# Forming the low halves of the first four units with TensorE and ScalarE, loading early on one queue, and ordering the first ten units anew

## The chip, the core and the metric

The kernel runs on one core of a Trainium2 chip. The metric is device time in microseconds (us), from three timed runs of the kernel before; beside it stands one profiled execution, whose rows are read below. TensorE multiplies matrices into PSUM, VectorE (DVE in the rows) and ScalarE (ACT) work element by element and can read PSUM, GpSimd (POOL) works on SBUF only, SyncE (SP) issues transfers.

## What is computed

A recurrent attention over 768 steps feeds two dense blocks in a row. All matrix products are asked for in float32 quality.

```python
for t in range(S):                       # B 4, H 8, S 768, D 48
    cur = einsum('bhd,bhe->bhde', u * k[t], v[t])
    y[t] = einsum('bhd,bhde->bhe', r[t], state + cur)
    state = w[t][..., None] * state + einsum('bhd,bhe->bhde', k[t], v[t])
x = y as (B*S = 3072 tokens, 384)
h = x @ w_in                             # 384 x 1024
solu = h * softmax(h)
ln = (solu - mean) / sqrt(var + 1e-6) * g_ln
x2 = ln @ w_out                          # 1024 x 384
out = leaky_relu(x2 @ w_in2, 0.01) @ w_out2   # 384 x 2048, 2048 x 384
```

## The kernel before

The 3072 tokens are 24 units of 128 tokens; unit i is the batch row i % 4 in the chunk i // 4 of the sequence. Each unit passes through three stages. The attention: `prep1` to `prep4`, `prep_k`, `prep_diag` on VectorE make decayed keys and queries, `prep_bonus`, `prep_vd`, `prep_state` on GpSimd the rest, `att_kt`, `att_scores`, `att_u`, `att_y` are small matmuls, and `att_x` (L624, L625) adds up the unit's activations x. The first dense layer: x is turned by TensorE (`x_t`, L630), then split into a high half (`x_hi`, L635, a ScalarE copy of PSUM to float32r) and a low half (`x_lo`, L639, VectorE: PSUM minus the high half), and multiplied in three passes per slice, high by high, high by low, low by high (`mm1`, L647, 9 matmuls of 512 columns for each half of the 1024 columns, into the one PSUM tile PH). The activation: `soft_max` (L652), `soft_e` (L655), `soft_z` (L659), which is the last reader of PH, `soft_nm` (L663, GpSimd), `soft_c` (L667), `soft_q` (L670); z is turned (`z_t`, L677, into PZ) and split in two halves (`z_hi`, L686, ScalarE; `z_lo`, L690, VectorE, 512 columns each). Groups of three units go through the second layer (`mm2a`, `mm2b`, L700; `mm2_out`, L705). From unit 4 on each unit carries one such product of an earlier group, so units 0 to 3 have less TensorE work than the rest.

The weights arrive as 64-bit floats and are decoded to float32 on the chip: for each of 14 slices of the first block, `w1_a` (L195 on VectorE, L197 on ScalarE), `w1_e` (L201), `w1_f` (L206), `w1_h` (L212), `w1_b` (L217), all VectorE. `w1_c` copies the high half (L783) and forms the difference in PSUM by an identity matmul (L785) and a matmul with minus the identity (L786); `w1_d` (L792) copies it out. This decoding runs between the first six units; the second block's weights follow later.

Nothing orders the work but the text: `FIRST` (units 0 to 9 and the weights), `LOOP` (units 10 to 13) and `LAST` are lists of step names, run in that order, and each engine executes its own instructions in the order in which they were issued. SyncE issues the loads of keys, queries and decays (`load_tr`, L460, two buffers), of values (`load_nat`, L466 and L467), of the second weight (`load_o`, L725) and of u and g. ScalarE issues the three loads of the first weight (`load_w1`, L715) at the start. `minus` is minus the identity, `ident` the identity. After the last unit the second block runs over 512-token groups (`mm3`, L895; `mm4`, L924).

Of the kernel before, what the change touches and what calls it, by code (L numbers as in the profile page):

```python
# [50 lines left out]
att_scores 3; x_hi 2; w1_a; w1_d; w1_f; w1_a; x_lo 2; soft_c 1; w1_e; soft_q 1; w1_h; prep_k 4; w1_b; prep3 4; mm1 2
0; w1_e; mm1 2 1; w1_c; w1_h; w1_f; w1_b; w1_h; z_t 1; att_kt 4; w1_d; w1_f; w1_b; z_hi 1 0; att_evac_s 3; load_nat
5; prep_check 4; w1_a; z_lo 1 0; att_evac_k 4; prep4 4; prep1 5; w1_c; prep_state 5; z_hi 1 1; prep_vd 3; att_u 4;
prep_k 5; w1_h; att_scores 4; z_lo 1 1; w1_d; soft_max 2; att_y 3; w1_c; soft_e 2; att_kt 5; w1_d; att_mid 4; att_x
3; x_t 3; att_mul_next 4; w1_b; prep_bonus 4; x_hi 3; soft_z 2; x_lo 3; prep2 5; w1_c; mm1 3 0; att_evac_s 4;
soft_nm 2; w1_e; att_state 4; w1_f; soft_c 2; w1_h; z_t 2; prep_diag 4; soft_q 2; z_hi 2 0; mm1 3 1; w1_b; z_hi 2 1;
att_evac_k 5; prep_vd 4; w1_d; load_tr 6; z_lo 2 0; w1_c; load_nat 6; att_u 5; prep_check 5; z_lo 2 1; att_y 4;
w1_d; prep3 5; prep4 5; att_scores 5; prep1 6; att_mid 5; mm2a 4; att_x 4; soft_max 3; prep_k 6; prep2 6; x_t 4;
load_tr 7; prep_bonus 5; soft_e 3; soft_z 3; x_hi 4; x_lo 4; mm2b 4; att_mul_next 5; prep_diag 5; soft_nm 3; mm1 4
0; mm2_out 4; soft_c 3; z_t 3; att_state 5; prep3 6; att_kt 6; prep_vd 5; att_evac_k 6; load_nat 7; prep1 7; prep_k  # L60
7; z_hi 3 0; att_evac_s 5; z_hi 3 1; prep_check 6; prep2 7; z_lo 3 0; z_lo 3 1; prep4 6; prep_state 6; mm2a 5; mm1 4
1; soft_max 4; prep_bonus 6; soft_q 3; prep_bonus 7; soft_e 4; load_tr 8; att_y 5; att_u 6; prep_check 7; att_x 5;
att_mid 6; att_scores 6; att_evac_s 6; att_kt 7; x_t 5; att_evac_k 7; mm2b 5; x_hi 5; soft_z 4; x_lo 5; soft_nm 4;
soft_c 4; prep3 7; att_mul_next 6; mm1 5 0; z_t 4; prep1 8; prep_diag 6; z_hi 4 0; z_lo 4 0; z_hi 4 1; prep_state 7;
att_state 6; prep4 7; prep_check 8; load_nat 8; prep_vd 6; mm1 5 1; mm2_out 5; z_lo 4 1; att_scores 7; att_u 7;
soft_max 5; att_y 6; prep2 8; prep_diag 7; att_x 6; att_evac_s 7; mm2a 6; soft_q 4; soft_e 5; x_t 6; prep_k 8;
att_mid 7; load_tr 9; soft_z 5; prep_bonus 8; x_hi 6; soft_nm 5; load_nat 9; soft_c 5; x_lo 6; prep3 8; mm2b 6;
prep4 8; mm2_out 6; att_mul_next 7; prep1 9; prep_vd 7; mm1 6 0; z_t 5; mm1 6 1; prep2 9; att_state 7; z_hi 5 0;
att_kt 8; z_lo 5 0; z_hi 5 1; mm2a 7; load_tr 10; z_lo 5 1; prep_diag 8; prep_k 9; att_evac_k 8; soft_max 6; att_y
7; att_u 8; load_nat 10; soft_q 5; prep_state 8; prep3 9; att_scores 8; att_kt 9; att_x 7; soft_e 6; x_t 7; att_mid  # L70
8; prep_bonus 9; x_hi 7; prep4 9; soft_z 6; prep_state 9; x_lo 7; mm2b 7; att_evac_k 9; mm1 7 0; att_mul_next 8;
att_evac_s 8; soft_nm 6; soft_c 6; z_t 6; soft_q 6; prep_vd 8; prep1 10; prep_diag 9; z_hi 6 0; mm1 7 1; z_lo 6 0;
prep_k 10; z_hi 6 1; att_state 8; mm2_out 7; att_u 9; prep_check 9; z_lo 6 1; att_scores 9; att_y 8; mm2a 8; att_mid
9; soft_max 7; soft_e 7; load_nat 11; att_x 8; x_t 8; x_hi 8; prep_check 10; prep_bonus 10; mm2b 8; soft_z 7; x_lo
8; mm1 8 0; prep2 10; prep_vd 9; soft_nm 7; prep3 10; att_mul_next 9; att_evac_s 9; prep_diag 10; load_tr 11; soft_c
7; prep1 11; z_t 7; prep4 10; att_kt 10; z_hi 7 0; att_evac_k 10; prep_k 11; z_hi 7 1; prep_bonus 11; z_lo 7 0; z_lo
7 1; mm1 8 1; att_state 9; soft_max 8; mm2_out 8; prep_state 10; load_tr 12; soft_q 7; soft_e 8; att_scores 10;
att_y 9; att_x 9; soft_z 8; prep2 11; att_u 10; att_evac_s 10; prep3 11; prep_vd 10; soft_nm 8; mm2a 9; soft_c 8;
att_mid 10; x_t 9; x_hi 9; load_nat 12; x_lo 9; prep_diag 11; mm2b 9; prep_check 11; att_mul_next 10; z_t 8; mm1 9
0; z_hi 8 0; z_lo 8 0; prep1 12; prep4 11; z_hi 8 1; prep_k 12; att_kt 11; mm2_out 9; att_evac_k 11; z_lo 8 1;  # L80
# [1011 lines left out]
```

## Time and profile before

| | us |
|---|---|
| median of three timed runs | 766.18 |
| lowest, highest | 765.87, 768.52 |
| the profiled execution, its own time | 766.61 |
| its span, first to last instruction | 764.9 |
| TensorE busy in the span | 722.2 (94%) |
| VectorE busy | 513.3 (67%) |
| ScalarE busy | 354.0 (46%) |
| GpSimd busy | 155.1 (20%) |

Busy time is an average over stages that differ: the first 100 us and the last 360 us have different limits. So the rows below are cut by stretch. A row of a timeline gives start, duration, engine, line and operation; on VectorE the next row usually starts 0.08 us before the end of the one before, so a step costs its duration less 0.08.

### The profile page before, as it was taken

The page shows a single profiled execution, that of the slowest core. Times are in us where ns is not written, and L with a number is a line of the kernel's source. Part 1 is how long each engine was busy: PE and PEld are TensorE (multiplying, and loading weights), DVE is VectorE, ACT ScalarE, POOL GpSimd, SP SyncE. Part 2 cuts the span into 40 slices and gives each one's busy share as a digit, 9 for nine tenths or more (in the row PEclk, how much of TensorE's full clock was granted, in tenths as well). Part 3 has the DMA queues.
Part 4 walks back from the last instruction along what each step waited for, and adds up shares of the span by engine and source line. Part 5 has one row for each costly group of instructions (what it writes and reads, how often), then busy time and mean ns, then how long its engine had stood idle before and what let it go on. Part 6 is the DMA issues. An engine that isn't in the chain of part 4 may idle for free.

```text
span 764.9 us, 14969 instructions
## 1 busy us (share of the span) xinstructions
PE 722.2 (94%) x6197; PEld 610.7 (80%) x6197; DVE 513.3 (67%) x866; ACT 354.0 (46%) x648; POOL 155.1 (20%) x181
## 2 busy tenths in 40 slices
PE   2588999999999999998999999999999999999996
PEld 1355878989998989887888888888888888888885
DVE  6999889778888888877989976353343334334332
ACT  3567565566565655566555544323322332332231
POOL 2331544355553444312000100001000100100000
PEclk9999999999999999999999999999999999999998
DMA  9652325353444443223363220040020001001001
GB/s 298 214 166 68 105 80 177 91 151 105 137 135 131 131 147 110 65 84 114 114 227 104 73 72 1 1 165 1 1 81 2 1 0 43 0 1 42 0 1 44
DMA packets 30189, 66.60 MB, mean 87 GB/s; under 512 B 3228, under 2 KB 15668, under 8 KB 29988
## 3 DMA queue, kind: packets, MB, share of 16 engines
q1 hardware_dynamic: 29300, 62.45, 25.9%
q10 hardware_dynamic: 816, 3.15, 1.2%
q8 instruction: 50, 0.82, 0.5%
q14 instruction: 23, 0.19, 0.1%
HBM read 56.13 MB, written 9.45 MB: 86 GB/s over the span
## 4 chain that ended last, share of the span: by engine, by line
PE 88%; DVE 7%; DMA 2%; issue 1%; ACT 1%; POOL 0%; ACTq 0%; DVEq 0%; POOLq 0%
PE PK L895 13%; PE PZ L895 13%; PE PH L647 12%; PE PO L700 11%; PE PA L924 9%; PE PH L924 9%; PE PO L924 4%; PE PZ L924 4%; PE PZ L677 2%; PE PZ L609 2%; PE PA L700 2%; DMA zh<-in_w1p_dram 2%; PE PA L546 2%; PE PZ L618 1%; PE PA L566 1%
## 5 line engine op out<-in xcount | busy, mean ns | idle before, releaser
L915 DVE TENSOR_TENSOR gw<-t,gh 128x512 fp32r<-128x512 f32 x96 | 68.4, 713 | 52.6 <-ACT gh L911 52.4
L911 ACT CAST gh<-t 128x512 fp32r<-128x512 f32 x96 | 59.6, 621 | 67.3 <-DVE t L907 51.5
L907 DVE TENSOR_TENSOR t<-t,PZ 128x512 f32<-128x512 f32 x48 | 32.9, 686 | 68.8 <-ACT t L903 68.6
L907 DVE TENSOR_TENSOR t<-t,PK 128x512 f32<-128x512 f32 x48 | 33.0, 687 | 60.0 <-ACT t L903 59.8
L881 POOL TENSOR_TENSOR x2l<-x2l,x2h 128x1536 fp32r<-128x1536 f32 x4 | 14.1, 3532 | 287.4 <-ACT x2h L877 287.4
L903 ACT ACTIVATE t<-PZ 128x512 f32<-128x512 f32 x48 | 28.7, 598 | 83.6 <-PE PZ L895 78.7
L903 ACT ACTIVATE t<-PK 128x512 f32<-128x512 f32 x48 | 28.7, 598 | 80.7 <-PE PK L895 76.4
L647 PE MATMUL PH<-w1ih,xh 128*128 128x512 f32 x144 | 58.7, 407 | 4.0 <-DVE zbuf L659 3.4
L700 PE MATMUL PO<-zh,w1oh 128*128 128x384 f32 x168 | 60.0, 357 | 0.0
L647 PE MATMUL PH<-w1ih,xl 128*128 128x512 f32 x144 | 57.3, 398 | 0.8 <-DVE xl L639 0.8
L647 PE MATMUL PH<-w1il,xh 128*128 128x512 f32 x144 | 56.8, 394 | 0.0
L700 PE MATMUL PO<-zh,w1ol 128*128 128x384 f32 x168 | 56.3, 335 | 0.0
L700 PE MATMUL PO<-zl,w1oh 128*128 128x384 f32 x168 | 56.3, 335 | 0.0
L895 PE MATMUL PK<-x2h,w2ih 128*128 128x512 f32 x144 | 56.2, 390 | 0.0
L895 PE MATMUL PZ<-x2h,w2il 128*128 128x512 f32 x144 | 56.1, 389 | 0.0
L895 PE MATMUL PZ<-x2l,w2ih 128*128 128x512 f32 x144 | 56.1, 389 | 0.0
L895 PE MATMUL PK<-x2h,w2il 128*128 128x512 f32 x144 | 56.0, 389 | 0.0
L895 PE MATMUL PK<-x2l,w2ih 128*128 128x512 f32 x144 | 56.0, 389 | 0.0
L895 PE MATMUL PZ<-x2h,w2ih 128*128 128x512 f32 x144 | 56.0, 389 | 0.0
L655 ACT ACTIVATE ebuf<-PH,nmax 128x1024 f32<-128x1024 f32 x24 | 26.8, 1117 | 38.9 <-DVE nmax L652 38.6
L652 DVE TENSOR_REDUCE nmax<-PH 128x1 f32<-128x1024 f32 x24 | 29.3, 1219 | 13.7 <-PE PH L647 13.6
L690 DVE TENSOR_TENSOR zl<-PZ,zh 128x512 fp32r<-128x512 f32 x48 | 31.8, 682 | 8.5 <-ACT zh L686 8.4
(183 smaller groups left out, 1943.2 us busy)
## 6 DMA issues: line engine op xcount, KB each, us to landing
tr<-in_trw_dram SPq DMA_DIRECT2D x23, 675.9 KB, 5.4
natq<-in_nat_q_dram SPq DMA_DIRECT2D x24, 384.0 KB, 5.3
w2s<-in_moe_w_in_dram SPq DMA_DIRECT2D x48, 128.0 KB, 2.2
w2s<-in_moe_w_out_dram SPq DMA_DIRECT2D x16, 384.0 KB, 3.1
...
```

What stands on the lines that cost most here:

```text
L546: pe.matmul(out=PA[64 * c:64 * c + 64, x, 64 * a:64 * a + 64], lhsT=kt[p:q, 2 * a + c], rhs=lt[p:q, 2 * a + c], start=True, stop=True)
L647: pe.matmul(out=PH[:, half], lhsT=a[:, kc], rhs=c[:, kc, 512 * half:512 * half + 512], start=(n == 0), stop=(n == 8))
L652: dve.tensor_reduce(out=nmax[:, i:i + 1], in_=flat(PH), axis=AX.X, op=ALU.max, negate=True)
L655: act.activation(out=ebuf, in_=flat(PH), func=AF.Exp, bias=nmax[:, i:i + 1], accum_out=s_all[:, i:i + 1])
L690: dve.tensor_tensor(out=zl, in0=p, in1=f(zh), op=ALU.subtract)
L700: pe.matmul(out=o2[m], lhsT=a[:, c, 128 * m:128 * m + 128], rhs=d[:, c], start=(c == 0 and q == 0), stop=(c == K1 - 1 and q == 2))
L895: pe.matmul(out=h_at[n % 2], lhsT=a[:, kc, 128 * o:128 * o + 128], rhs=d[:, kc], start=(q == 0), stop=(q == 8))
L903: act.activation(out=gs[n][0], in_=h_at[n % 2], func=AF.Copy, scale=0.01)
L907: dve.tensor_tensor(out=t, in0=t, in1=h_at[n % 2], op=ALU.max)
L911: act.copy(out=gh, in_=t)
L915: dve.tensor_tensor(out=gw, in0=t, in1=f(gh), op=ALU.subtract)
L924: pe.matmul(out=at, lhsT=a[:, c % 4, 128 * o:128 * o + 128], rhs=d, start=(c == 0 and q == 0), stop=(c == K2 - 1 and q == 2))
```

## The change

For units 0 to 3 (`N_PE` = 4) the low halves of x and z are no longer made by VectorE. After the high half is copied out, TensorE adds minus that half onto the turned values in PSUM (`x_lm`, one matmul of 384 columns; `z_lm`, one of 512 for each half), and ScalarE copies what is left to the low half. The turning matmuls get explicit start and stop flags so that their PSUM group can be added to. `prep_k` goes to GpSimd from unit 2 on instead of from unit 5 on. The loads of the first weight move from ScalarE's queue to SyncE's (`load_w`), the first of them ahead of unit 0's `load_tr`, and the `FIRST` order places all early loads. `load_tr` takes 1552 columns instead of 1545, cut at 528 instead of 521 for unit 0. `FIRST` has the same steps otherwise, in a new order.

```diff
+TRL = 1552
+N_PE = 4
 FIRST = """
-load_tr 1; prep1 0; prep2 0; w1_a; load_nat 0; prep3 0; prep_k 0; w1_e; load_u; w1_f; prep4 0; att_scores 0; w1_a;
-w1_a; w1_h; w1_e; prep_state 0; w1_e; w1_b; w1_f; w1_f; att_kt 0; w1_h; w1_c; prep1 1; w1_h; w1_b; prep_check 0;
-prep2 1; w1_b; prep3 1; w1_a; w1_a; w1_a; prep_k 1; w1_e; w1_e; att_evac_k 0; w1_d; prep_bonus 0; w1_f; att_u 0;
...
-prep_check 2; prep2 3; att_x 1; att_state 2; prep_bonus 2; w1_h; x_t 1; soft_max 0; x_hi 1; prep_diag 2; load_tr 4;
-soft_e 0; prep_vd 2; prep3 3; att_kt 3; prep_state 2; w1_g; soft_z 0; w1_f; load_nat 3; soft_nm 0; soft_c 0; x_lo 1;
...
+w1_a; prep1 0; load_w 1; prep_state 0; w1_e; prep2 0; load_w 2; load_tr 1; w1_f; prep_check 0; prep3 0; prep_k 0;
+w1_h; att_kt 0; prep4 0; w1_a; w1_a; w1_b; w1_e; w1_e; w1_f; w1_c; w1_d; att_evac_k 0; load_o 0; w1_f; w1_h; w1_h;
+w1_a; w1_a; w1_b; w1_e; w1_c; w1_b; w1_e; load_g; load_nat 0; load_u; att_u 0; w1_a; prep1 1; w1_f; load_nat 1;
...
+prep_vd 1; att_kt 2; load_nat 2; w1_d; prep_state 2; w1_a; mm1 0 1; att_evac_k 2; prep1 3; prep_check 3; att_y 1;
+att_u 2; prep4 2; soft_max 0; att_x 1; w1_e; load_tr 4; prep_k 3; soft_e 0; x_t 1; att_mid 2; att_scores 2; soft_z
+0; w1_f; att_evac_s 2; w1_g; w1_h; prep_bonus 2; x_hi 1; x_lm 1; x_lo 1; mm1 1 0; prep_check 4; w1_h; soft_nm 0; mm1
...
 """
-        def load_tr(i, eng, cuts=(0, TRW)):
-            t = ap2.tile([128, TRW], F32, name="tr", bufs=2)
+        def load_tr(i, eng, cuts=(0, TRL)):
+            t = ap2.tile([128, TRL], F32, name="tr", bufs=2)
...
-            (dve if i < 5 else pool).tensor_tensor(
+            (dve if i < 2 else pool).tensor_tensor(
...
+        def turn(out, x, n, of):
+            pe.matmul(out=out, lhsT=x, rhs=ident, is_transpose=True, start=(n == 0), stop=(n == of - 1),
+                      skip_group_check=True)
+
+        def x_lm(i):
+            pe.matmul(out=PZ[0][:, 0:384], lhsT=minus, rhs=flat(xhl[i][0]), start=False, stop=True,
+                      skip_group_check=True)
+
+        def z_lm(i, hb):
+            pe.matmul(out=PZ[hb], lhsT=minus, rhs=z_views(i, hb)[0], start=False, stop=True, skip_group_check=True)
...
-            dve.tensor_tensor(out=xl, in0=PZ[0][:, 0:384].rearrange("p (k t) -> p k t", k=KC), in1=f(xh),
-                              op=ALU.subtract)
+            p = PZ[0][:, 0:384].rearrange("p (k t) -> p k t", k=KC)
+            if i < N_PE:
+                act.copy(out=xl, in_=p)
+            else:
+                dve.tensor_tensor(out=xl, in0=p, in1=f(xh), op=ALU.subtract)
...
-            dve.tensor_tensor(out=zl, in0=p, in1=f(zh), op=ALU.subtract)
+            if i < N_PE:
+                act.copy(out=zl, in_=p)
+            else:
+                dve.tensor_tensor(out=zl, in0=p, in1=f(zh), op=ALU.subtract)
...
-        def load_w1():
-            for hf in range(2):
-                t = ma.tile([128, K1 * 384], I32, name="zl" if hf else "zh")
-                for a, n in ((0, 1), (1, 2)) if hf == 0 else ((0, 3),):
-                    act.dma_start(
...
+        def load_w(n):
+            hf, a, k = ((0, 0, 1), (0, 1, 2), (1, 0, 3))[n]
+            t = w1_at[hf] = w1_at.get(hf) or ma.tile([128, K1 * 384], I32, name="zl" if hf else "zh")
+            sp.dma_start(
...
-            load_tr(0, sp, (0, 521, TRW))
-            load_w1()
+            load_w(0)
+            load_tr(0, sp, (0, 528, TRL))
```

Two facts of the new order are used below, both read off the two lists. Up to and with `soft_z 3`, VectorE has 13 instructions fewer and none more: `x_lo` of units 0 to 3, `z_lo` of units 0 to 2 (two each) and `prep_k` of units 2 to 4. Up to and with `mm1 4 0`, TensorE has the same steps and ten more: `x_lm` of units 0 to 3 and `z_lm` of units 0 to 2 (two each).

## Rows read from the trace of the kernel before

**Rows 1.** Busy us by stretch: PE, PEld, DVE, ACT, POOL; granted clock, DMA share, GB/s.

```profile
13.10:51.90 38.80, 23.96 (x291) 15.22 (x287) 38.19 (x66) 20.94 (x43) 12.83 (x13) 1.00 0.63 217
51.90:98.00 46.10, 41.87 (x533) 32.82 (x533) 41.32 (x78) 30.36 (x61) 13.77 (x19) 0.93 0.32 98
98.00:168.60 70.60, 69.06 (x969) 61.49 (x969) 59.67 (x91) 42.25 (x83) 32.96 (x42) 1.00 0.39 121
168.60:400.00 231.40, 228.46 (x2805) 204.27 (x2805) 195.43 (x339) 133.79 (x253) 78.53 (x89) 1.00 0.41 127
400.00:764.90 364.90, 357.80 (x1579) 295.94 (x1577) 172.28 (x283) 124.27 (x207) 14.13 (x4) 0.99 0.10 34
```

**Rows 2.** The chain that ended last, 50 to 101 us: start, us, what.

```profile
50.62 1.21 DVE zbuf L659 x2
51.87 0.73 PE PH L647 x2
...
58.66 2.09 PE PH L647 x9
...
98.06 2.33 PE PH L647 x9
```

**Rows 3.** Timeline of VectorE, 6 to 14 us, the rows that waited for transfers.

```profile
6.00 1.24 DVE L478 TENSOR_TENSOR_SCAN suf<-tr,sel 112x520 f32<-112x520 f32 x1 [3.81 <-DMA tr<-in_trw_dram]
...
9.60 0.69 DVE L489 TENSOR_TENSOR kt<-tr,suf 112x512 f32<-112x512 f32 x1 [0.68 <-DMA tr<-in_trw_dram]
...
13.02 0.43 DVE L195 TENSOR_SCALAR ebuf<-zh 128x512 int32<-128x512 int32 x1 [1.06 <-DMA zh<-in_w1p_dram]
```

**Rows 4.** Timeline of VectorE, 38 to 69 us: `x_lo`, `z_lo`, `prep_k`, their successors.

```profile
38.03 0.55 DVE L639 TENSOR_TENSOR xl<-PZ,xh 128x384 fp32r<-128x384 f32 x1
38.50 0.20 DVE L484 RECIPROCAL e<-suf 112x8 f32<-112x8 f32 x1
...
59.70 1.29 DVE L690 TENSOR_TENSOR zl<-PZ,zh 128x512 fp32r<-128x512 f32 x2 [0.72 <-ACT zh L686]
60.90 1.22 DVE L652 TENSOR_REDUCE nmax<-PH 128x1 f32<-128x1024 f32 x1
...
68.72 0.69 DVE L489 TENSOR_TENSOR kt<-tr,suf 112x512 f32<-112x512 f32 x1
```

**Rows 5.** Groups by line and form, 0 to 98 us: busy us, mean ns | idle before.

```profile
L667 ACT ACTIVATE zbuf<-zbuf,nm_all 128x1024 f32<-128x1024 f32 x3 | 3.4, 1149 | 2.4 <-POOL nm_all L663 2.4
L686 ACT CAST zh<-PZ 128x512 fp32r<-128x512 f32 x6 | 3.3, 592 | 0.2 <-PE PZ L677 0.2
L635 ACT CAST xh<-PZ 128x384 fp32r<-128x384 f32 x5 | 2.4, 474 | 1.2 <-PE PZ L630 1.2
L489 POOL TENSOR_TENSOR kt<-tr,suf 112x512 f32<-112x512 f32 x2 | 2.4, 1184 | 3.7 <-PE PZ L609 3.7
```

**Rows 6.** Stretches of the start, columns as in rows 1; GB/s is last.

```profile
0.00:2.50 2.50, 0.00 (x0) 0.00 (x0) 1.11 (x4) 0.26 (x1) 1.64 (x10) 1.00 0.17 25
2.50:5.00 2.50, 0.00 (x0) 0.00 (x0) 0.00 (x0) 1.42 (x3) 1.20 (x7) 1.00 0.92 287
5.00:7.50 2.50, 0.00 (x0) 0.00 (x0) 1.47 (x3) 0.00 (x0) 0.00 (x0) 1.00 1.04 349
7.50:10.00 2.50, 0.00 (x0) 0.00 (x0) 1.82 (x3) 0.72 (x1) 0.00 (x0) 1.00 1.04 305
...
10.00:20.00 10.00, 4.57 (x39) 2.43 (x39) 8.90 (x16) 3.53 (x7) 1.68 (x2) 1.00 1.02 364
...
37.50:40.00 2.50, 2.11 (x13) 1.45 (x9) 2.50 (x6) 1.36 (x3) 0.52 (x1) 1.00 1.02 394
```

**Rows 7.** Timeline of VectorE and GpSimd, 25 to 30 us: one step with and without GpSimd.

```profile
25.88 0.42 DVE L206 TENSOR_SCALAR zl<-zl 128x512 int32<-128x512 int32 x1
...
29.08 1.00 POOL L521 TENSOR_TENSOR natq<-natq 128x384 f32<-128x384 f32 x1
29.25 1.11 DVE L206 TENSOR_SCALAR zl<-zl 128x512 int32<-128x512 int32 x1
```

More of the change, by code (lines that the diff above doesn't have):

```diff
@@ L51 @@
[L51 to L80, printed above, removed]
@@ new lines @@
+prep_k 4; att_x 2; att_state 2; att_evac_k 3; w1_c; x_t 2; soft_e 1; att_u 3; load_tr 5; x_hi 2; prep2 4; att_mid 3;
+x_lm 2; x_lo 2; soft_z 1; mm1 2 0; prep_bonus 3; att_evac_s 3; w1_d; att_kt 4; soft_nm 1; w1_a; w1_f; w1_h; soft_c
+1; w1_e; w1_b; w1_h; w1_c; z_t 1; att_mul_next 3; load_nat 4; w1_a; w1_f; prep3 4; w1_d; mm1 2 1; soft_q 1; z_hi 1
+0; w1_h; att_evac_k 4; w1_b; prep1 5; prep4 4; z_lm 1 0; att_state 3; prep_k 5; prep_diag 3; z_hi 1 1; w1_c; z_lm 1
+1; prep_vd 3; soft_max 2; att_u 4; att_mid 4; att_mul_next 4; z_lo 1 0; z_lo 1 1; att_y 3; w1_d; att_scores 4; w1_b;
@@ new lines @@
+soft_e 2; w1_c; att_x 3; x_t 3; x_hi 3; prep_bonus 4; att_kt 5; soft_z 2; att_state 4; prep2 5; w1_e; w1_f; w1_h;
+x_lm 3; soft_nm 2; x_lo 3; soft_c 2; load_tr 6; att_evac_k 5; w1_a; w1_d; w1_b; mm1 3 0; w1_e; w1_f; z_t 2; w1_c;
+z_hi 2 0; w1_h; prep3 5; z_lm 2 0; w1_b; att_evac_s 4; mm1 3 1; prep4 5; z_hi 2 1; w1_d; z_lm 2 1; w1_c; z_lo 2 0;
+prep_diag 4; z_lo 2 1; load_nat 5; att_u 5; prep1 6; soft_max 3; w1_d; att_y 4; prep_vd 4; att_x 4; att_scores 5;
+prep_state 5; prep2 6; soft_q 2; att_mid 5; prep_bonus 5; soft_e 3; prep_check 5; mm2a 4; soft_z 3; soft_nm 3; x_t
@@ new lines @@
+4; x_hi 4; mm2b 4; att_mul_next 5; soft_c 3; prep3 6; load_nat 6; x_lo 4; mm1 4 0; prep4 6; prep_k 6; z_t 3; att_kt
+6; z_hi 3 0; att_evac_s 5; z_lm 3 0; z_hi 3 1; prep_diag 5; mm1 4 1; load_tr 7; mm2_out 4; z_lm 3 1; prep1 7; prep_k
+7; mm2a 5; att_scores 6; soft_max 4; prep_check 6; z_lo 3 0; z_lo 3 1; prep_vd 5; load_nat 7; prep2 7; prep3 7;
+prep_bonus 6; att_state 5; att_evac_k 6; load_tr 8; att_y 5; prep_state 6; soft_q 3; att_u 6; prep_diag 6; soft_e 4;
+prep_bonus 7; att_x 5; soft_z 4; prep4 7; att_mid 6; soft_nm 4; att_kt 7; x_t 5; mm2b 5; prep_vd 6; att_mul_next 6;
@@ new lines @@
+x_hi 5; x_lo 5; mm1 5 0; prep1 8; prep_check 7; soft_c 4; soft_q 4; att_evac_s 6; z_t 4; load_nat 8; prep_diag 7;
+mm1 5 1; z_hi 4 0; prep_vd 7; prep_k 8; z_hi 4 1; att_evac_k 7; z_lo 4 0; prep2 8; att_state 6; z_lo 4 1; load_tr 9;
+att_y 6; att_u 7; mm2_out 5; soft_max 5; prep_state 7; att_scores 7; att_x 6; att_kt 8; soft_e 5; x_t 6; prep_bonus
+8; mm2a 6; att_mid 7; prep3 8; soft_z 5; att_mul_next 7; soft_nm 5; x_hi 6; prep_state 8; att_evac_k 8; x_lo 6;
+load_nat 9; mm1 6 0; mm2b 6; prep_check 8; prep1 9; prep2 9; soft_c 5; soft_q 5; z_t 5; z_hi 5 0; prep4 8;
@@ new lines @@
+prep_bonus 9; att_evac_s 7; z_hi 5 1; z_lo 5 0; load_tr 10; mm1 6 1; mm2_out 6; att_state 7; z_lo 5 1; soft_max 6;
+att_u 8; att_y 7; att_scores 8; prep3 9; soft_e 6; att_x 7; prep4 9; prep_k 9; mm2a 7; prep_check 9; prep_diag 8;
+prep_diag 9; x_t 7; soft_z 6; load_nat 10; att_mid 8; mm2b 7; x_hi 7; x_lo 7; soft_nm 6; load_tr 11; soft_c 6; mm1 7
+0; att_mul_next 8; att_evac_s 8; z_t 6; prep_vd 8; z_hi 6 0; prep_state 9; att_state 8; att_kt 9; prep1 10; z_lo 6
+0; z_hi 6 1; prep_k 10; z_lo 6 1; mm1 7 1; soft_max 7; att_y 8; prep_state 10; soft_q 6; mm2_out 7; att_scores 9;
@@ new lines @@
+att_evac_k 9; prep2 10; att_x 8; prep_vd 9; att_u 9; soft_e 7; att_mid 9; att_kt 10; x_t 8; x_hi 8; att_mul_next 9;
+mm2a 8; soft_z 7; att_evac_k 10; att_state 9; x_lo 8; soft_nm 7; soft_c 7; prep_check 10; prep1 11; att_evac_s 9;
+mm1 8 0; z_t 7; mm1 8 1; z_hi 7 0; prep3 10; z_lo 7 0; z_hi 7 1; z_lo 7 1; soft_q 7; att_y 9; prep_bonus 10; att_u
+10; prep_check 11; prep_k 11; prep_diag 10; prep4 10; prep2 11; att_scores 10; prep3 11; mm2b 8; prep_state 11;
+soft_max 8; att_x 9; load_nat 11; load_tr 12; x_t 9; soft_e 8; soft_z 8; att_mid 10; mm2_out 8; att_evac_s 10;
@@ L82 @@
+att_kt 11; att_mul_next 10; soft_nm 8; mm2a 9; x_hi 9; prep4 11; x_lo 9; prep1 12; soft_c 8; soft_q 8; mm1 9 0; z_t
+8; prep_check 12; prep_bonus 11; prep_vd 10; load_nat 12; prep2 12; prep_k 12; mm2b 9; z_hi 8 0; z_hi 8 1;
+prep_bonus 12; load_tr 13; prep_diag 11; z_lo 8 0; att_state 10; mm1 9 1; mm2_out 9; z_lo 8 1; att_evac_k 11;
+prep_vd 11
 """
```

39 lines of the change are left out of this document (18 added, 21 removed).

## The prediction

> **What bounds the kernel now.** I read the stretches first, because a share of the whole span would mislead: TensorE is 94% busy in it, and yet the first 98 us are something else. From 98 us on TensorE works 69.06 of 70.60 us, then 228.46 of 231.40, then 357.80 of 364.90, nearly all at full granted clock [rows 1]. Nothing that is saved or lost before 98 us is given back later: there is no idle time worth naming for it to vanish into. So the question is when TensorE reaches the state that it has at 98 us in the kernel before, and what it still has to do from there.
>
> Before that VectorE is the full engine: 38.19 of 38.80 us from 13.1 to 51.9 us, 41.32 of 46.10 from there to 98 [rows 1]. The chain of waits says how the two are coupled. `soft_z` of unit 0 on VectorE ends at 51.83 us and releases `mm1 1 0` at 51.87 [rows 2], since PH has one copy. The same coupling sits at 98.06 us: that group of nine is `mm1 4 0`, which follows `soft_z 3`. I take it as the landmark. From 51.9 to 98 us most pieces of the chain are TensorE's, though, and its clock averaged 0.93 there, that is, some of the stretch ran at the lower level of 1.2 GHz [rows 1]. So VectorE is the main limit, with TensorE close behind; this doubt becomes a rival.
>
> **What VectorE loses.** Up to `soft_z 3` the new list has 13 VectorE instructions fewer and none more. `x_lo` starts at 38.03 and its successor at 38.50: 0.47 us a step, four times, 1.9 us. Two `z_lo` in a row take from 59.70 to 60.90: 0.60 each, six times, 3.6 us. `prep_k` lasts 0.69, less the overlap of 0.08 that the `x_lo` pair shows, 0.61, three times, 1.8 us [rows 4]. Together 7.3 us. VectorE is 92% to 98% busy until then, so I count them in full: -7.3.
>
> **What the start gains.** VectorE first works on data at 6.00 us, after 3.81 us of waiting for unit 0's decays; then it waits 0.68 us for the keys and 1.06 us for the second weight slices [rows 3]. Moved data by time: 0.06 MB at 2.5 us, 0.78 at 5.0, 1.65 at 7.5, 2.42 at 10 and 6.06 at 20 [rows 6]. In the new order the first 0.52 MB are weight slice 0 and the next 0.24 MB unit 0's decays: 0.76 MB, moved by about 5.0 us. Before, the same two pieces shared the engines from two queues and VectorE started about 1 us after that much was moved; with the same 1 us the decays are there at 5.9, as before, but slice 0 comes earlier and `w1_a` fills 0.34 us of the wait. The keys end at 1.22 MB (about 7.3 us with the 1 us), slices 1 and 2 at 2.27 MB (about 10.5). VectorE wants the keys at about 9.4 us and slices 1 and 2 at 11.2, when it has done 5.5 us of steps; before, it got there at 13.02 with 4.9 us done. That is 2.4 us. If slices 1 and 2 were no earlier than now it would be 0.6; if nothing at all waited, 3. I take -2.4. The price is that unit 0's values and queries, now loaded early, come behind 6.1 MB, at about 21 to 23 us. `att_u 0` waits for them on TensorE, ahead of `att_scores 0`; `att_evac_s 0` on VectorE needs both and stands after 21.9 us of VectorE's steps, near 28 us. I cost this at nothing while the transfers run as before. That they share one queue doesn't slow them in these rows: from 37.5 to 40 us, with SyncE's queue alone at work, 394 GB/s were moved [rows 6].
>
> **What goes to GpSimd.** Three `prep_k` of 1.18 us each [rows 5], on an engine that was busy 13 of 46 us [rows 1]. The cost is on VectorE: `w1_f` took 0.42 us alone and 1.11 us while GpSimd multiplied [rows 7], 0.7 us more. Met by about half of the three, that is +1.0; zero if they meet steps that don't slow, 2.1 if each of the three meets such a step once. The Trainium skill (SBUF — State Buffer, section Who interferes with whom) goes further: VectorE and GpSimd share a pair of ports as an exclusive lock, and who comes second waits for the whole instruction. By it the sum would have 3.5 here in place of 1.0; the 1.11 us row shows a delay of most of GpSimd's remaining 0.83 us, so the row leans to the page.
>
> **What ScalarE and TensorE get.** ScalarE copies four times 384 and, before the landmark, six times 512 columns out of PSUM: 0.47 and 0.59 us by the copies of the high halves [rows 5], 5.4 us. It was busy 30.36 of 46.10 us [rows 1], so I cost the work itself at nothing; if ScalarE's queue were full it would cost those 5.4 us. TensorE gets ten matmuls before the landmark, at most 0.23 us each (nine of 512 columns take 2.09 [rows 2]), 2.3 us, under VectorE's cover: 23.96 us busy of 38.80, then 41.87 of 46.10 [rows 1]. If that cover is gone they count in full. The two `z_lm 3` lie after the landmark, where TensorE is full: +0.5.
>
> **Waits.** Each `z_lm` stands in TensorE's queue and waits for a ScalarE copy; behind it are `w1_c`, `att_y` and `mm1` of the next unit, and VectorE's `att_x` and `soft_max` wait for those. On the other side VectorE's own 0.72 us wait for `z_hi` [rows 4] goes. VectorE idled 4.8 us from 51.9 to 98 us [rows 1]; the order of units 0 to 3 is new, so that sum can be anything from 0 to twice as much. I take -0.7, with -4.8 and +4.8 as ends. After the landmark TensorE idled 1.5 us up to 168.6 [rows 1]. The new order of units 4 to 9 is a bit tighter in two places: `mm1 8 0` has only `att_y 8`, `att_scores 9`, `att_u 9`, `att_kt 10`, `x_t 8` and `mm2a 8` to cover the softmax of unit 7, without `mm2b 8`. I take +1.0, ends -1.5 and +5 (1 us a unit).
>
> **The sum.** -7.3 - 2.4 + 1.0 + 0.5 - 0.7 + 1.0 = -7.9 us. The profiled execution took 766.6 us, so 758.7; it lies 0.4 above the median of the timed runs, so 758 for that. The landmark would move from 98.1 to about 88.7 us, ahead of the last two terms.
>
> **Rivals.** First, TensorE paces the stretch from 51.9 us on, as its share of the chain [rows 2] and the lower clock [rows 1] suggest. Then only what lies before `soft_z 0` counts: the start's 2.4, `x_lo 0` and two `prep_k` (1.7), and 2.7 us of other VectorE steps that the new list puts behind `soft_z 0`; less 2.3 + 0.5 for the matmuls and 1.0 for units 4 to 9, and nothing else. A gain of 3.0: 763. Against it: TensorE is 91% busy there with waits and the lower clock counted in, and TensorE's waits were for VectorE at 51.87.
>
> Second, the new order also closes what VectorE waited for: all 4.8 us, and the start's full 3. Then 7.3 + 3 + 4.8 - 1.5 = 13.6: 753. For it: a list made of the same steps with less VectorE work has more room.
>
> Third, slower: ScalarE's queue becomes the path. Each of the 12 low halves is now a link through ScalarE and TensorE in order. If each copy finds one pass such as `soft_c` ahead of it, 1.15 us [rows 5], and TensorE stands meanwhile, 13.8 us are added to the 7.9 gained: 772. It turns into a loss from 0.66 us each on. Against it: ScalarE is idle a third of the time there, and TensorE has slack.
>
> Fourth, GpSimd's lock holds VectorE for every `prep_k` in full, 3.5 in place of 1.0: 761. [...]
>
> **How the numbers follow.** Forecast 0.50; TensorE paces 0.20; everything closes 0.15; ScalarE's queue 0.08; the lock 0.07. Predicted is the forecast's 758. The range reaches from 752 (below the second rival) to 766 (above the first, with about half of the ends of the waits); left out are the third rival and the tails of the others, 2 in 10. What a measurement of this kernel can tell from no change is about 0.5%, 3.8 us, so faster means below 762.4. Forecast, second and fourth rival lie there but for a tail, and a little under half of the first: 0.74. Same 0.18, slower 0.08.
>
> **What would show it.** In the profile of the changed kernel: `mm1 4 0`, the ninth group of nine at PH, starts near 89 us and not 98; VectorE's rows for the low half of z fall from 48 to 40 and of x from 24 to 20; GpSimd's `kt` rows rise from 19 to 22; the wait before the second `w1_a` is gone; TensorE is 97% or more busy from the landmark on. I am wrong if VectorE's idle time before the landmark grows by more than 7 us, if TensorE idles over 5 us between the landmark and `mm1 9 1`, or if transfers of unit 0 hold `att_u 0` beyond 28 us.

## The result and the profile after

| | before | after |
|---|---|---|
| median of the timed runs, us | 766.66 (4 runs) | 759.96 (4 runs, 758.74 to 760.47) |
| the profiled execution, its own time | 766.61 | 760.32 |
| its span | 764.9 | 758.6 |

After to before is 0.9907, with a 95% interval of 0.9884 to 0.9930: 0.9% faster. The forecast was 758 us, the gain 6.3 to 6.7 us where 7.9 were summed.

The stretches of the kernel after, cut at the points that answer to those of [rows 1] (columns as there):

```profile
13.10:46.00 32.90, 26.38 (x308) 15.95 (x307) 28.68 (x49) 18.70 (x39) 13.28 (x12) 1.00 0.72 230
46.00:92.00 46.00, 43.09 (x555) 33.87 (x556) 44.35 (x82) 35.22 (x71) 20.22 (x24) 1.00 0.37 107
92.00:162.00 70.00, 68.92 (x967) 60.86 (x967) 56.06 (x84) 43.71 (x86) 39.98 (x43) 1.00 0.44 130
162.00:400.00 238.00, 235.08 (x2833) 209.82 (x2834) 202.25 (x353) 135.31 (x254) 76.31 (x86) 1.00 0.41 124
400.00:758.60 358.60, 351.43 (x1549) 290.42 (x1548) 165.95 (x269) 121.18 (x202) 14.12 (x4) 0.99 0.10 33
```

From 46 to 92 us TensorE and VectorE are both 94% to 96% busy, and the granted clock is 1.00 where it was 0.93 [rows 1]. From 92 us on TensorE is 98% busy, as before. One thing about this column matters further down: time for which the trace holds no record of the clock counts as 1.00. The records begin at 34.3 us in the kernel after and at 29.5 us in the kernel before, so the 1.00 of the first row, and of the first row of [rows 1], says nothing about the time ahead of that.

The table gives the places at which the kernels of this study are compared, read from their timelines (us): the starts of `soft_z` of units 0 to 3, the landmark `mm1 4 0`, and the end of `mm1 9 1`. From there to the end of the span it is 594.6 to 596.6 us in all 14 traces, so whatever a kernel gains or loses is fixed at that point, to about 1 us either way. A trace is one execution, and it can lie up to 2 us from the median of its kernel (more_vectore: 764.67 against 762.77).

| | soft_z 0 | soft_z 1 | soft_z 2 | soft_z 3 | mm1 4 0 | end of mm1 9 1 | median |
|---|---|---|---|---|---|---|---|
| before | 50.62 | 64.59 | 82.91 | 96.68 | 98.06 | 168.63 | 766.66 |
| after | 47.62 | 61.39 | 74.47 | 87.38 | 90.74 | 162.00 | 759.96 |
| low_halves_back | 46.15 | 63.85 | 80.30 | 95.20 | 97.99 | 169.36 | 766.13 |
| low_halves_alone | 51.25 | 68.59 | 90.21 | 110.04 | 111.42 | 184.19 | 781.98 |
| checks_moved | 51.16 | 69.47 | 90.03 | 107.39 | 108.77 | 181.50 | 779.63 |
| ring_closed_early | 50.66 | 68.56 | 88.46 | 105.12 | 106.50 | 179.20 | 777.19 |
| loads_alone | 52.21 | 65.96 | 83.21 | 97.01 | 98.39 | 168.94 | 765.82 |
| prep_k_back | 47.51 | 62.40 | 75.39 | 88.29 | 91.65 | 162.68 | 760.65 |
| links_held | 47.65 | 62.14 | 76.13 | 89.97 | 93.34 | 164.31 | 760.66 |
| more_vectore | 48.79 | 64.11 | 78.06 | 92.59 | 94.86 | 166.97 | 762.77 |
| more_tensore | 46.30 | 60.71 | 75.84 | 89.58 | 92.94 | 163.95 | 761.25 |
| more_tensore_before | 51.07 | 67.56 | 87.49 | 102.14 | 103.52 | 174.15 | 770.49 |
| y0_first | 48.70 | 62.48 | 75.56 | 88.48 | 91.84 | 162.87 | 759.53 |
| w1_c_behind_x | 49.65 | 63.43 | 76.53 | 89.41 | 92.77 | 163.67 | 761.10 |

VectorE's start in the kernel after, which answers to [rows 3] (start, duration, engine, line, operation; in brackets the wait):

```profile
5.16 0.43 DVE L199 TENSOR_SCALAR ebuf<-zh 128x512 int32<-128x512 int32 x1 [2.97 <-DMA zh<-in_w1p_dram]
6.11 1.24 DVE L482 TENSOR_TENSOR_SCAN suf<-tr,sel 112x520 f32<-112x520 f32 x1 [0.53 <-DMA tr<-in_trw_dram]
...
9.46 0.67 DVE L493 TENSOR_TENSOR kt<-tr,suf 112x512 f32<-112x512 f32 x1
...
11.25 0.42 DVE L199 TENSOR_SCALAR ebuf<-zh 128x512 int32<-128x512 int32 x1
```

The second `w1_a` starts at 11.25 us without a wait; the forecast had 11.2 and before it was 13.02 [rows 3]. The landmark, from the timeline of the kernel after:

```profile
87.38 1.22 DVE L677 SCALAR_TENSOR_TENSOR zbuf<-PH,ebuf 128x1024 f32<-128x1024 f32 x1
88.33 0.49 PE L632 MATMUL PZ<-ident,x 128*128 128x128 f32 x3
88.57 0.42 PE L721 MATMUL PO<-zh,w1oh 128*128 128x384 f32 x1
...
90.74 0.39 PE L665 MATMUL PH<-w1ih,xh 128*128 128x512 f32 x1
```

`soft_z 3` is done at 88.6 us, but `mm1 4 0` no longer starts with it, as it did in [rows 2]: TensorE still has `x_t 4` and `mm2b 4` (12 matmuls, 88.57 to 90.7) ahead of it. VectorE gained 9.3 us up to here, the landmark 7.3.

### The profile page after: what moved, and what is told of

It is laid out like the page before. It is cut to its first block, busy times and chain, and to the rows that moved or that the text cites. A ratio compares the mean times of both kernels' runs of the same rounds, so it can differ in the third digit from the quotient of the medians.

```text
span 758.6 us, 15011 instructions
## 1 busy us (share of the span) xinstructions
PE 726.3 (96%) x6209; PEld 612.0 (81%) x6209; DVE 505.8 (67%) x851; ACT 359.5 (47%) x660; POOL 166.7 (22%) x184
## 4 chain that ended last, share of the span: by engine, by line
PE 81%; DVE 12%; ACT 2%; DMA 2%; issue 1%; POOL 1%; SPq 0%; DVEq 0%; ACTq 0%; POOLq 0%
PE PK L915 12%; PE PZ L915 12%; PE PH L665 11%; PE PO L721 10%; PE PA L944 8%; PE PH L944 8%; PE PO L944 4%; PE PZ L944 4%; PE PZ L632 3%; PE PZ L613 2%; PE PA L721 2%; DMA tr<-in_trw_dram 1%; PE PA L550 1%; PE PZ L622 1%; PE PO L805 1%
## 5 line engine op out<-in xcount | busy, mean ns | idle before, releaser
L493 POOL TENSOR_TENSOR kt<-tr,suf 112x512 f32<-112x512 f32 x22 | 28.7, 1305 | 42.6 <-DVE suf L482 26.0
```

The lines of the kernel that those rows point to most:

```text
L493: (dve if i < 2 else pool).tensor_tensor(out=kt[0:112], in0=trs[i][0:112, 521:1033].rearrange("p (c t) -> p c t", c=8), in1=suf[i][0:112, ...
```

## The experiments

The first question was whether VectorE's steps count in full up to the landmark, or whether TensorE paces from about 52 to 60 us on (the first rival). Each change is to the kernel named in its expectation; times are medians, with the kernel before at 766.0 to 767.0 us beside them.

### low_halves_back: VectorE forms the low halves again

```diff
-N_PE = 4
+N_PE = 0
-... x_lm 0; ... z_lm 0 0; z_lm 0 1; ...   (all twelve taken out of the list)
```

> The changed kernel, with its order and its early transfers, but the low halves of x and z of units 0 to 3 are subtracted by VectorE again (ten matmuls and twelve ScalarE copies gone). 'VectorE paces up to the landmark': ten steps before soft_z 3 come back to VectorE, 4 x 0.47 + 6 x 0.60 = 5.5 us, all of it late: about 765.5 us, the landmark mm1 4 0 at 96 us. 'TensorE paces from about 60 us': VectorE's 5.5 us find slack and TensorE is relieved of 2.8 us of matmuls: 757 to 760 us, landmark at 88 to 91. 'Both are full by turns' (VectorE's soft_z 3 was done 2.1 us before the landmark in the changed kernel): 5.5 - 2.1 = 3.4 late, 0.5 given back by z_lm of unit 3: about 763 us, landmark at 94.

Twelve matmuls go, not ten: ten ahead of the landmark and two behind it. 766.13 us; to before 0.9997 (0.9982 to 1.0011). All of the gain is gone: the new order, the new transfers and GpSimd's three `prep_k` are worth nothing measurable without the low halves. Ten steps of 5.5 us made 6.2 us of difference, the "VectorE paces" case in size. But the way was not that of VectorE alone. The stretches of this run:

```profile
46.00:92.00 46.00, 39.69 (x439) 30.33 (x440) 41.03 (x78) 26.63 (x51) 12.44 (x17) 0.85 0.25 71
...
65.00:70.00 5.00, 4.78 (x16) 3.66 (x16) 5.00 (x13) 2.84 (x4) 0.67 (x2) 0.66 0.00 0
...
75.00:85.00 10.00, 8.67 (x99) 7.20 (x99) 7.53 (x16) 3.75 (x7) 2.86 (x4) 0.66 0.34 101
```

VectorE was 89% busy from 46 to 92 us, less than in the kernel after. TensorE was 86% busy and its clock was granted at 0.85, in some stretches at 0.66, that is, partly at 1.2 GHz; in the kernel after it was 1.00. `mm1 1 0` lasted 4.94 us here and 2.35 us there: about half of the difference is a wait for `x_lo 1` ahead of its third matmul, the other half is the spacing of its matmuls, 0.43 us here and 0.23 there. So part of the 6.2 us may be TensorE's slower clock and not VectorE's steps.

How much it may be can be read off the kernel before. Its 68 executions beside the experiments took 764.3 to 766.1 us where the mean granted clock of the whole span was 0.997 or more (16 of them), and 767.1 to 769.5 us where it was 0.990 or less (13). The kernel after had 0.997 to 0.999 in all four executions, low_halves_back 0.989 to 0.994 in all twelve. Against the 16, whose median is 765.4, the kernel after is still 5.4 us faster. A line through the 68 gives 0.43 us for 0.001 of clock; by it the step from 0.992 to 0.997, the two medians, is about 2 of the 6.2 us. That is an estimate, and it doesn't say whether the lower clock caused the waits or came of them.

### more_vectore: a scan done twice

```diff
+            if 2 <= i < 7:
+                dve.tensor_tensor_scan(...)      (prep1 once more, same operands)
```

> The changed kernel with VectorE's first scan (prep1, 1.24 us, 1.15 beyond its overlap) done twice for units 2 to 6: 5.8 us more on VectorE before the landmark, nothing else changed. 'VectorE paces': landmark at 96.5, 765.8 us. 'TensorE paces from about 60 us': the scans of units 2 and 3 (2.3 us) lie before that and count, the rest is hidden: 762 us. 'Both by turns': 5.8 less the 2.1 us that lie between soft_z 3 and the landmark, 763.7 us.

762.77 us, 2.8 more than the changed kernel; in the trace, which is the slowest of the ten executions, the end of `mm1 9 1` is 5.0 us later. 5.8 us more on VectorE cost about half of that by the medians: not "in full". "Both by turns" (763.7) and "TensorE paces from about 60 us" (762) can't be told apart by it. The granted clock from 46 to 92 us was 0.93 and not 1.00, so the clock may have a part in the 2.8 too.

### more_tensore and more_tensore_before: matmuls done twice

```diff
-            pe.matmul(out=d, lhsT=ident, rhs=t, start=True, stop=False)
-            pe.matmul(out=d, lhsT=minus, rhs=hi, start=False, stop=True)
+            for _ in range(2 if key[0] == "o" and key[1] < 6 else 1):
+                pe.matmul(out=d, lhsT=ident, rhs=t, start=True, stop=False)
+                pe.matmul(out=d, lhsT=minus, rhs=hi, start=False, stop=True)
```

> The changed kernel with the two matmuls of w1_c done twice for the first six slices of the second weight: by the spacing of a pair in the trace (0.84 to 0.95 us and its tail) about 6 x 1.0 = 6 us more on TensorE between 54 and 80 us. 'VectorE paces': TensorE has 46 - 43.1 = 2.9 us of idle time from 46 to 92 us to take them, so 3 us late at most: 760 to 763 us. 'TensorE paces': 766 us.

> The kernel before (766.1 us) with the two matmuls of w1_c done twice for the first six slices of the second weight, as in more_tensore: about 6 us more on TensorE ahead of the landmark. 'VectorE paces the kernel before': TensorE was busy 38.9 of 46 us from 46 to 92 and takes them in its idle time: 766 to 768 us. 'TensorE paced it from 51.9 us on', the first rival of the prediction: 772 us. 'Both by turns', as the changed kernel showed with 3.5 of 6 us between soft_z 0 and the landmark: 769 us.

In both traces each of the six repetitions ends 0.85 us after the first time: 5.1 us more work, a little less than the 6 expected. In the kernel after: 761.25 us, 1.3 more, 2.0 at the end of `mm1 9 1`; this lies in the range of "VectorE paces" (760 to 763), and by the intervals (0.9916 to 0.9961 here, 0.9884 to 0.9930 there) the 1.3 can't be told from nothing. From `soft_z 0` to the landmark, where the added work lies, it took 46.6 us and not 43.1, so 3.5 more; that execution had been 1.3 us earlier at `soft_z 0`, which takes back part of it. In the kernel before: 770.49 us, ratio 1.0041 (1.0027 to 1.0055), 3.8 us more, 5.5 at `mm1 9 1`. It is not the clock that makes this difference: two executions with a mean granted clock of 0.996 took 769.4 and 769.7 us, the kernel before at 0.997 took 764.7 to 766.1 (13 executions). So TensorE was close to being the limit in the kernel before, too, between "both by turns" (769) and "TensorE paced it" (772).

### low_halves_alone, checks_moved, ring_closed_early: the low halves in the old order

```diff
-... x_lo 0; ... z_lo 0 0; z_lo 0 1; ...
+... x_lm 0; x_lo 0; ... z_lm 0 0; z_lo 0 0; z_lm 0 1; z_lo 0 1; ...   (units 0 to 3, old list)
```

> The kernel before, with its order, its loads and its prep_k, and only the low halves of x and z of units 0 to 3 formed by TensorE and copied by ScalarE; each new matmul stands right ahead of the low half's copy. 'VectorE paces': ten steps of 5.5 us fewer before soft_z 3, 0.5 lost behind the landmark: 761.5 us, landmark at 92.5. 'TensorE paces from 52 us on': only x_lo 0 (0.5 us) comes early and 2.8 us of matmuls are added: about 769 us. 'An order made for the other split of work wastes it': half of the 5.5, 764 us.

781.98 us, ratio 1.0199 (1.0174 to 1.0224): 15.9 us slower than before, beyond every theory that I had named for this run. It is the kind of loss that the prediction's slower rival described, and larger: that rival put 13.8 us on the links, and against the 761.5 that the saved steps were to give, 20.5 us were lost here. VectorE's waits from 13.1 to 112 us, the five largest (engine, tile, line, for whom; us in total, times, longest):

```profile
DVE ao L580 <- PE PA L548: 10.2, 2, 7.8
DVE x L626 <- PE PZ L620: 6.0, 2, 3.7
DVE ebuf L197 <- DMA zh<-in_w1p_dram: 2.5, 1, 2.5
DVE ss L557 <- PE PA L548: 2.1, 1, 2.1
DVE nmax L668 <- PE PH L663: 1.8, 1, 1.8
```

With the smaller ones they add up to 24.2 us, where the kernel before has 6.0 up to 98 us. The 18.2 us more, less the 5.5 us of steps saved, are about the 13.4 us by which the landmark is late. The longest, 7.78 us ahead of `att_mid 5` at 106.15, is followed back in the timelines of TensorE and ScalarE:

```profile
100.33 0.40 PE L638 MATMUL PZ<-zh,minus 128*128 128x512 f32 x1
100.76 0.59 ACT L707 CAST zl<-PZ 128x512 fp32r<-128x512 f32 x1 [0.87 <-PE PZ L638]
101.25 0.54 ACT L802 CAST w1oh<-zl 128x384 fp32r<-128x384 f32 x1
101.69 0.72 ACT L474 ACTIVATE junk<-tr,blo 112x512 bf16<-112x512 f32 x1
...
102.81 0.50 PE L638 MATMUL PZ<-zh,minus 128*128 128x512 f32 x1
...
103.35 0.59 ACT L707 CAST zl<-PZ 128x512 fp32r<-128x512 f32 x1
...
103.98 0.24 PE L601 MATMUL PZ<-zero 48*64 48x192 bf16 x1 [0.48 <-ACT zl L707]
...
105.35 0.24 PE L548 MATMUL PA<-lt,kt 48*64 48x64 f32 x2
```

`z_lm 2 0` (L638) waits its turn behind `mm1 3 1`; then the copy (L707); then `z_lm 2 1`; then its copy, behind `prep_check 5` (L474) in ScalarE's queue; only then is PZ free for `att_y 4` (L601), and `att_scores 5` (L548), for which VectorE waits, is behind that. In the kernel before `z_lo` was one VectorE step behind `z_hi`, with no turn on TensorE. Two kernels then moved the parts of that ring:

```diff
 checks_moved        ... z_hi 2 0; ... z_lo 2 0; z_lo 2 1; prep_check 5; ...  (3, 4 behind units 0, 1)
 ring_closed_early   ... z_hi 2 0; z_hi 2 1; z_lm 2 0; z_lm 2 1; mm1 3 1; z_lo 2 0; z_lo 2 1; soft_q 2; ...
                     (units 0, 1 likewise; soft_q 2 stood ahead of mm1 3 1)
```

> The low halves alone in the order of the kernel before (which took 782.0 us) with one thing changed in ScalarE's queue: prep_check of units 3, 4 and 5, 1.66 us each, are issued behind the two low halves of z that they stood ahead of. In the run without this, VectorE waited 7.78 us for att_mid 5, because att_y 4 and att_scores 5 on TensorE stood behind z_lo 2 1, and that behind prep_check 5 in ScalarE's queue. 'ScalarE's queue became the path': up to 3 x 1.66 = 5.0 us earlier, about 777 us, and VectorE's wait for att_mid 5 falls to about 6. 'The matmuls z_lm stand too late in TensorE's queue': ScalarE only waits elsewhere, 780 to 782 us.

> The kernel checks_moved (779.6 us: the low halves in the order of before, without prep_check in their way) with each z_lm issued right behind the z_hi that it waits for, ahead of w1_c, att_u, att_scores and mm1 3 1 on TensorE, and z_lo right behind on ScalarE. 'Where the two steps of the low half stand in the two in-order queues holds PZ, and with it att_y and all behind it': VectorE's waits for att_mid 4, att_x 3 and att_mid 5 (13.9 us in low_halves_alone) shrink to half or less, 772 us or lower. 'The low halves cost that much wherever they stand': 778 to 780 us.

779.63 and 777.19 us: 2.4 us from ScalarE's queue, 2.4 more from the places of `z_lm`, `z_lo` and `z_hi`. The intervals of neighbours overlap (1.0174 to 1.0224, 1.0131 to 1.0207, 1.0107 to 1.0153); only the two steps together, 4.8 us, are clear of noise. Both expectations (777, and 772 or lower) were too good, and ring_closed_early came out next to the other theory, that "the low halves cost that much wherever they stand" (778 to 780). VectorE's wait for `att_mid 5` fell from 7.8 to 5.3 and 4.6 us. So the places in the two queues are shown for about a third of the 15.9 us; what the other 10.5 us against before consist of is not settled. In ring_closed_early VectorE still waits in eight places of 0.9 to 4.6 us between 50 and 113 us, and low_halves_alone had a granted clock of 0.82 from 46 to 92 us, 0.66 from 50 to 60 and 0.62 from 80 to 90, where before had 0.93 in the whole stretch. The mean clock doesn't account for the 10.5 us, though: three executions of ring_closed_early with 0.993 or 0.994 took 776.1 to 776.9 us, the kernel before at the same clock (15 executions) 765.3 to 767.6.

### links_held: the slower rival's price in the new order

```diff
-... prep_check 3; ... prep_check 4; ... prep_check 5; ...
+... prep_check 3; z_lo 0 0; ... prep_check 4; z_lo 1 0; ... prep_check 5; z_lo 2 0; ...
```

> The changed kernel (760.0 us) with prep_check of units 3, 4 and 5, 1.66 us each on ScalarE, issued right ahead of the first low half of z of units 0, 1 and 2: each of these three links between TensorE and ScalarE is held for 1.66 us, more than the 1.15 us that the prediction's slower rival put there, and ScalarE's work stays the same. 'The new order leaves the links slack' (in it z_lo follows z_hi by 1.7 to 2.4 us already, and x_t, att_y of the next unit stand a good way behind): 760 to 761 us. 'Each link holds TensorE, as the slower rival has it': 3 x 1.66 = 5.0 us, 765 us, with VectorE waiting for att_x or att_mid behind it. In the order of before taking the same three steps out of the links was worth 2.4 us.

760.66 us: 0.7 more than the changed kernel by the medians, 2.3 at the end of `mm1 9 1` in the one trace, and not 5.0. In that trace the low halves of unit 2 were copied 3.2 us later than in the kernel after (whose row is the last):

```profile
84.06 0.72 ACT L476 ACTIVATE junk<-tr,blo 112x512 bf16<-112x512 f32 x1
...
85.62 1.05 ACT L709 CAST zl<-PZ 128x512 fp32r<-128x512 f32 x2

82.39 1.11 ACT L709 CAST zl<-PZ 128x512 fp32r<-128x512 f32 x2
```

In the new order the links have most of the slack that they would need; in the old one, taking the same three steps out of the links was worth 2.4 us of 5.0.

### loads_alone and prep_k_back: the smaller parts

```diff
 loads_alone (to before)
-            load_tr(0, sp, (0, 521, TRW)); load_w1()
+            load_w(0); load_tr(0, sp, (0, 528, TRL))
-load_tr 1; prep1 0; ...
+load_w 1; load_w 2; load_tr 1; prep1 0; ...
 prep_k_back (to after)
-            (dve if i < 2 else pool).tensor_tensor(
+            (dve if i < 5 else pool).tensor_tensor(
```

> The kernel before, with its order, in which only the early transfers are changed: weight slices 0 to 2 on SyncE's queue, slice 0 ahead of unit 0's decays, slices 1 and 2 and the second halves ahead of load_tr 1. Predicted for the start was 2.4 us in all, of which 0.34 needed a w1_a moved into the first wait. 'The start counts in full': the second w1_a no longer waits 1.06 us, the keys may come later as they stand behind slice 0; 764 to 765 us. 'Other waits swallow it', as decays of unit 1 and unit 0's values now come behind all weight slices: 766 or more.

765.82 us, ratio 1.0002 (0.9986 to 1.0018): nothing. The rows of VectorE's start in loads_alone say why:

```profile
11.16 0.43 DVE L197 TENSOR_SCALAR ebuf<-zh 128x512 int32<-128x512 int32 x1
...
18.98 1.24 DVE L480 TENSOR_TENSOR_SCAN suf<-tr,sel 112x520 f32<-112x520 f32 x1 [3.38 <-DMA tr<-in_trw_dram]
```

The second `w1_a` is 1.9 us earlier than before, and then `prep1 1` waits 3.38 us for the decays of unit 1, which now come behind all weight slices. The new order has other steps in that place: there `prep1 1` starts at 19.02 without a wait.

> The changed kernel with prep_k of units 2 to 4 on VectorE again, as before. 'VectorE paces': three steps of 0.61 us come back and about 1.0 us of slowing by GpSimd goes: +0.8, 760.8 us. 'TensorE paces': no difference, 760. 'The shared port holds VectorE for every prep_k in full' (3 x 1.18 us): 3.5 - 1.8 = 1.7 us earlier, 758.3.

760.65 us, ratio 0.9927 (0.9908 to 0.9946): the 758.3 of the theory that the port holds VectorE for every `prep_k` in full lies outside the interval (758.3 to 766.1 is 0.9898), and 760.8 and 760 can't be told apart.

### y0_first and w1_c_behind_x: can the wait at 34 us be had?

In the kernel after VectorE had one long wait before the landmark:

```profile
29.00 2.07 PE L805 MATMUL PO<-zl,ident 128*128 128x512 f32 x2 [0.68 <-ACT w1il L812]
...
34.15 0.56 DVE L628 TENSOR_TENSOR x<-PZ,vd 128x384 f32<-128x384 f32 x1 [3.66 <-PE PZ L622]
```

`att_y 0` stands behind that `w1_c`. The two kernels move it.

```diff
 y0_first
-... w1_c; att_y 0; ... att_x 0; w1_e; w1_c; prep_state 1; w1_b; x_t 0; ...
+... att_y 0; w1_c; ... w1_e; w1_b; att_x 0; w1_c; prep_state 1; x_t 0; ...
 w1_c_behind_x
+... att_y 0; ... w1_e; w1_b; att_x 0; prep_state 1; x_t 0; prep1 2; att_scores 1; w1_c; ... x_lm 0; w1_d; w1_c; ...
```

> The changed kernel with two moves in its list: w1_c, which stood ahead of att_y 0 on TensorE and took 29.0 to 31.5 us, goes behind it, and w1_e and w1_b (1.1 us on VectorE) go ahead of att_x 0, where VectorE waited 3.66 us at 34.15. 'VectorE paces': about 1.3 + 1.1 = 2.4 us earlier at soft_z 0, and as much at the end: 757.6 us. 'TensorE paces from about 60 us': the head start is lost by the landmark, 759 to 760 us.

> The changed kernel with the fourth and fifth w1_c moved behind att_scores 1 and x_lm 0 on TensorE (in y0_first they stood ahead of att_u 1 and x_t 0 and cost VectorE 3.81 us of waiting for att_evac_s 1, as much as was won ahead of att_x 0), and w1_e and w1_b on VectorE ahead of att_x 0. 'VectorE's waits at the start are what can be won': 2 us earlier at soft_z 0 and 1 to 2 at the end, 758 to 759 us. 'The head start is lost by the landmark, where TensorE has no idle time': 760 us.

759.53 and 761.10 us: no gain that can be told from the changed kernel's 759.96. The wait moved both times (the last row gives the stretch of y0_first from 30.8 to 37.6 us, columns as in [rows 1]):

```profile
32.38 0.56 DVE L628 TENSOR_TENSOR x<-PZ,vd 128x384 f32<-128x384 f32 x1 [0.36 <-PE PZ L622]
...
39.58 0.74 DVE L559 COPY_PREDICATED ss<-mask,PA 128x512 f32<-128x512 int32 x1 [3.81 <-PE PZ L636]

32.40 2.07 PE L805 MATMUL PO<-zl,ident 128*128 128x512 f32 x2
30.80:37.60 6.80, 6.80 (x72) 4.06 (x68) 4.50 (x8) 1.46 (x3) 4.28 (x4) 0.50 0.79 288
```

In y0_first (above) `att_x 0` waits 0.36 us and `att_evac_s 1`, seven microseconds later, 3.81. The two `w1_c` that stand ahead of it began at 32.40 and 35.86 us, with the granted clock at 0.50, and took 2.5 and 2.2 us; in the kernel after the `w1_c` at 34.62 us, with the clock at 1.00, took 1.5. By these rows the lower clock is, as an estimate, some 1.6 us of the 3.81. In w1_c_behind_x (below) it is `soft_max 0`, whose second half of columns needs the weight slices that were put off:

```profile
46.51 1.22 DVE L670 TENSOR_REDUCE nmax<-PH 128x1 f32<-128x1024 f32 x1 [5.45 <-PE PH L665]
```

Before `soft_z 0` the decoding of the six slices, TensorE's queue and VectorE's steps are tied together, so a step moved ahead of one puts another behind, and the clock comes on top: its records begin at 27.4 us in y0_first, with 0.50 from 30.8 to 37.6, and only at 40.2 in w1_c_behind_x. No kernel of this study beats the changed one by more than its measurement can tell.

## Why the prediction came out right, point by point

**Where the gain is made.** Right: TensorE is 98% busy from the landmark on, and the rest of the span is the same in all traces to about 1 us either way, so 7.3 us at the landmark became 6.6 at `mm1 9 1` and 6.3 in the profiled time.

**What VectorE loses, with the start and GpSimd.** The sum up to the landmark was -9.4. `soft_z 3` starts 9.3 us earlier. The rows that were to show it do: the low half of z has 40 VectorE rows (L711) and that of x 20 (L658), GpSimd's `kt` 22. That the sum is so close is luck, though. The stretches up to the start of `soft_z 3`, after and before (columns as in [rows 1]):

```profile
0.00:87.38 87.38, 66.27 (x841) 46.55 (x842) 77.06 (x139) 56.30 (x113) 32.64 (x48) 1.00 0.56 179
0.00:96.68 96.68, 66.13 (x848) 48.53 (x849) 84.58 (x153) 52.88 (x107) 29.44 (x47) 0.96 0.52 168
```

VectorE's busy time fell by 7.5 us where -7.3 and +1.0 were summed, its idle time by 1.8 where the start's 2.4 and the waits' 0.7 were. Two misses of about 1.2 us cancel: the slowing by GpSimd doesn't show in the total, and the waits did not shrink.

**The landmark.** This step failed by 2 us: it was forecast at 88.7 and is at 90.74. I had let the landmark follow `soft_z 3` as in [rows 2]; with VectorE that much earlier, TensorE's own queue is what it follows. That is the first rival, setting in at the end of the stretch. more_tensore_before shows that TensorE had been nearer to the limit in the kernel before than the 0.20 for that rival suggests: 5.1 us more matmuls cost 3.8 us there. The clock of 0.93 in [rows 1] was a sign of it that I priced too low.

**After the landmark.** +1.5 was summed (matmuls of `z_lm 3`, tighter units 4 to 9); it was 0.7 up to `mm1 9 1`, with TensorE idle 1.1 us from 92 to 162 us, 0.7 of it once, for `att_x 5`. This term was too large by 0.8 and gave back part of the 2 us: luck again, as the two errors have nothing to do with each other.

**The terms are not terms.** This was wrong in the working, though the sum was close. The low halves were put at -5.5 of the -7.3. With the new order they are worth 6.2 us (low_halves_back), with the old one they make the kernel 15.9 slower (low_halves_alone). The start was put at -2.4; with the old order it is worth nothing (loads_alone). The order as such was put at about zero, and together with the loads and `prep_k`, without the low halves, it comes to that: low_halves_back has `soft_z 0` 4.5 us earlier than the kernel before and the landmark at the same place. But it is what lets the other parts count. The expectations of low_halves_alone (761.5) and loads_alone (764 to 765) rested on the same adding up and missed.

**The third rival** (ScalarE's queue becomes the path, 772, chance 0.08) did not come about, and links_held shows the slack that kept it away. Its chance was judged by ScalarE's idle third; where the links stand in the two queues mattered more. In the old order the same links came with a loss of 15.9 us with ScalarE 61% busy from 46 to 92 us; moving them in the queues gave back 4.8 of it, and the rest is open.

**GpSimd.** The price of +1.0 can't be measured (prep_k_back); the fourth rival's 3.5 is excluded. The rows of the kernel after show both sides, VectorE's and GpSimd's timeline:

```profile
39.07 1.06 DVE L199 TENSOR_SCALAR w2s<-zh 128x384 int32<-128x384 int32 x1
39.09 0.83 POOL L536 TENSOR_TENSOR vd<-natv,dg 128x384 f32<-128x384 f32 x1
...
41.71 0.34 DVE L199 TENSOR_SCALAR w2s<-zh 128x384 int32<-128x384 int32 x1
...
43.11 0.67 DVE L509 TENSOR_TENSOR lt<-tr,e 112x512 f32<-112x512 f32 x1
43.33 1.48 POOL L493 TENSOR_TENSOR kt<-tr,suf 112x512 f32<-112x512 f32 x1 [3.41 <-issue]
```

At 39.07 VectorE's step lasts 1.06 us (the same step at 41.71, with GpSimd idle, 0.34): it waits, while GpSimd's `prep_k`, begun at 37.94, runs to 39.13 and `prep_vd` behind it to 39.92. At 43.33 it is GpSimd's `prep_k` that waits, 1.48 against 1.18 us, behind `prep4 3`, which began first and kept its 0.67. Of the five `prep_k` on GpSimd before 92 us three were stretched so (1.48, 1.49, 1.67), and in each a VectorE step with both operands in SBUF had begun before. The fourth rival had VectorE wait each time; its 3.5 us hold only if GpSimd comes first at each of the three. The Trainium skill (SBUF — State Buffer, section Who interferes with whom) has it that the order of issue decides who blocks, and that a VectorE step with two SBUF inputs contends as well; the 1.48 us row agrees with that, and the rival had left it out.

**`att_u 0`** was forecast at 21 to 23 us and starts at 22.77. What I did not see is that `att_y 0`, behind two `w1_c`, would hold VectorE 3.66 us at 34.15. VectorE's idle time up to the landmark stayed about the same in all: 0.6 and 4.8 us in the first two stretches of [rows 1], 4.2 and 1.7 in those of the kernel after. So the -0.7 for the waits was not earned, as the stretches above show.
